# Feed-forward groups in alternating weight order with tiles shared at borders, and Strassen in all second products of layer 2

## The chip, the cores and the metric

One core of a Trainium2 chip (trn2). The metric is device time in microseconds (us) of one execution. TensorE (PE) multiplies, VectorE (DVE) and ScalarE (ACT) work on tiles of 128 partitions, GpSimd (POOL) is idle in the part in question, and SyncE (SP) issues the DMA transfers. Each engine runs its own instructions in the order in which the program was built and waits where an operand or a buffer is not ready.

## The reference, cut to what matters

```
attn = softmax(q k^T / 8 + decay, causal) v      # 4 batches x 8 heads, 576 x 64
x = attn as [2304 tokens, 512]
h = x @ w_in                                     # 512 -> 2048, layer 1
x = (h * sigmoid(1.702 h)) @ w_out               # 2048 -> 512
g = x @ w_gate; v = x @ w_val                    # 512 -> 1536, layer 2
out = (g * sigmoid(g) * v) @ w_out2              # 1536 -> 512
```

All tensors are fp32. Every fp32 operand of a product is split into a high part (a cast to fp32r) and the low rest (a subtraction), and a product is three matmuls: high x high, high x low, low x high.

## The kernel before

**Tiles and stages.** Attention comes first (to about 210 us). The feed-forward part follows: 2304 tokens in three groups of 768, each as two halves of N = 384 columns. Layer 1 has 8 units of 256 hidden columns, layer 2 has 6 units, each with a gate and a value part. Every first product of a unit is one *chain*: the seven products of Strassen-Winograd's scheme, each of six matmuls of 128x128 by 128x384 (lines 750 to 752). The products accumulate in three PSUM tiles called c1, b2 and b3: a new chain's b2 is seeded by an ACT copy of c1 (line 779). PSUM banks are named bank or, where one tile holds two of them, xx.

**The operands of a chain.** X holds the seven forms of a group's input. At the border from one group to another `xbuild` loads eight blocks, makes the sums with 8 DVE subtractions (line 711) and then the 14 high parts on ACT (line 724) and 14 low parts on DVE (line 725). `stream` loads the two weight tiles of a chain, A (384 KB) and B (512 KB), into one of two buffers each (wA, wB), with a cast on ACT (line 684) and a subtraction on DVE (line 685). The weights in memory were prepared before by `prepare` (lines 616 to 651; line 616 is its first ACT step): each unit once, ranked AHEAD (100) before the unit's first use.

**What follows a chain.** `gate` and `value` collect c1, b2, b3 with ACT copies (line 770), DVE additions (line 773), Silu on ACT (lines 813 to 821) and products on DVE (lines 832 to 836). `rounded` splits the result into high and low parts (lines 841 and 842).

**The second products.** They run for a pair of units. `second` is plain: 8 products of 12 matmuls (lines 898 to 900), 96 in all, added into eight fp32 accumulators (line 908 for the first pair, 911 after it). `strassen` does the same by seven products for each of two column blocks: 14 products of 6 matmuls (lines 943 to 945), 84 in all, gathered in PSUM tiles t1, t3, t2 and added by DVE (lines 956 to 960). For it `rounded` first makes the seven forms with four DVE subtractions (line 859) and then splits 7 forms instead of 4. Layer 1 is always plain. In layer 2 group 0 is plain (WHOLE = 1), groups 1 and 2 use Strassen. The weights of the second products come by DMA into a ring of four tiles, wo.

**The order.** A *run* is a stretch of units of one layer and group. Layer 1 goes through the groups twice (units 0 to 3 of groups 0, 1, 2, then units 4 to 7 of 0, 1, 2). Layer 2 has group 0 units 0 to 3, group 1 units 0 to 5, group 2 units 0 to 5, group 0 units 4 and 5. That makes 10 runs and 9 borders. Units always go upward, so the first weights of a run are not those that its predecessor ended with. A group that is left and taken up again has its accumulators saved to memory (yd in layer 1, od in layer 2) and loaded again. The positions of the products in PE's queue come from the patterns ZPAT, WPAT and ZEND; second products start GLAG (plain) or GLAG2 (Strassen) after the pair's last chain. `Program.order` then plans all operations with durations and ranks and emits them in the order of their planned starts, which fixes each engine's queue.

```
    chains = [(1, g, u, "w1") for ps in range(2) for g in range(NG3) for u in range(ps * U1 // 2, (ps + 1) * U1 // 2)]
    runs = [(0, range(0, 4)), (1, range(U2)), (2, range(U2)), (0, range(4, U2))]
    chains += [(2, g, u, k) for g, us in runs for u in us for k in ("wg", "wv")]
```

Of the kernel before, what the change touches and what calls it, by code (L numbers as in the profile page):

```python
# [20 lines left out]
KD = 4  # L21
# [14 lines left out]
DMA_ISSUE, SLACK = 400, 2000  # L36
# [4 lines left out]
EARLY, AHEAD = 8, 100  # L41
SEED, WHOLE = 6, 1
# [3 lines left out]
NB_, NG3 = 384, 3  # L46
# [128 lines left out]
def kernel(  # L175
# [380 lines left out]
    def plain(lay, g):  # L556
        return lay == 1 or g < WHOLE
# [100 lines left out]
    def stream(kind, u, part, rank, stage=None):  # L658
        if part not in ("A", "B"):
            j = ring_of("wO", len(wo))  # L660
            wslot[kind, u, part] = j
            if kind == "w2o":
# [10 lines left out]
        j = ring_of("w" + part, len(ws))  # L673
        wslot[kind, u, part] = j
        if stage is None:
# [122 lines left out]
    def gate(lay, g, u, pos, half):  # L798
        w = 4 if plain(lay, g) else 7
        b_ = buffer(half, w)  # L800
# [44 lines left out]
    def rounded(lay, g, u, t):  # L845
        b_, at_ = made[lay, g, u]
        r = rk(t) - 40
# [131 lines left out]
    for i in range(2, len(chains) + 1):  # L979
        lead1 = i < len(chains) and chains[i][0] == 1  # L980
        whole = not lead1 and chains[min(i, len(chains) - 1)][1] < WHOLE
        pat = (1, -5, 0, 2, -3, 0, 6, -4, 0, 7, 0) if lead1 else WPAT if whole else ZEND if i > len(chains) - 5 else ZPAT
        for m in pat:
# [5 lines left out]
            else:  # L989
                j = i if m > 0 else i - 1  # L990
                if 2 <= j < len(chains):
# [3 lines left out]
                    if m == -4 and kind != "wg" and u % 2:  # L995
# [8 lines left out]
    for i, (lay, g, u, kind) in enumerate(chains):  # L1004
        need.setdefault((kind, u), pos[i][1])
        if kind != "wg" and u % 2:
            for k in range(2):
                need.setdefault(("w1o" if lay == 1 else "w2o", u - k), placed[i][0])
# [15 lines left out]
    for i, (lay, g, u, kind) in enumerate(chains):  # L1024
        events.append((pos[i][1], 2, "chain", i))
        if kind != "wg":
            events.append((pos[i][4] + MP, 1, "round", i))
            if u % 2:
# [3 lines left out]
    def group(lay, g, u, *_):  # L1032
        return lay, g, u >= 4 if lay == 1 or g == 0 else False

    groups = list(dict.fromkeys(group(*c) for c in chains))

# [26 lines left out]
    for t, _, what, arg in events:  # L1063
        if what == "chain":
            lay, g, u, kind = chains[arg]
            gi = groups.index(group(lay, g, u))
# [4 lines left out]
            else:  # L1071
                early = u % 4 < 2 if lay == 1 else u < (2 if g == 0 else 3) or u == 4 and g == 0
# [95 lines left out]
```

## Time and profile before

| what | value |
| --- | --- |
| median of 3 runs | 1009.05 us (1008.55 to 1009.98) |
| the profiled execution's own time | 1006.06 us |
| its span in the trace | 1004.4 us |
| PE busy | 969.6 us (97%), 6593 matmuls |
| DVE busy | 804.3 us (80%) |
| ACT busy | 583.6 us (58%) |
| POOL busy | 120.8 us (12%), all of it in attention |

The span is what the trace covers; the execution's own time has 1.66 us more around it, and the median lies 2.99 us above that execution. Sums on rows of the trace are made against 1006.06. Busy time of an engine is the sum of its instructions without overlaps. An idle stretch in brackets says how long the engine stood still just before an instruction, and which event ended it. What a stall costs is seen from start to start of matmuls, since the matmul after a stall takes longer and the one behind it starts later.

### The profile page before, as it was taken

What the parts mean: (1) busy time and instruction counts of PE and PEld (TensorE: products, weight loads), DVE (VectorE), ACT (ScalarE), POOL (GpSimd) and SP (SyncE); (2) the same over time, 40 slices, a digit from 0 to 9 for tenths busy, and PEclk for the clock granted to TensorE, in tenths of its full rate; (3) what the DMA queues carried; (4) which work ended last, traced back from release to release, by engine and by line L of the source; (5) the groups of instructions that cost most, each with busy time, mean ns of one, the idle gap of its engine ahead of it and who ended that gap; (6) DMA issues with size and microseconds to landing.
All of it is one profiled execution on the core that took longest, in us unless ns stands there. A gap on an engine that the chain in (4) does not pass through costs nothing.

```text
span 1004.4 us, 18051 instructions
## 1 busy us (share of the span) xinstructions
PE 969.6 (97%) x6593; PEld 908.1 (90%) x6593; DVE 804.3 (80%) x1509; ACT 583.6 (58%) x1017; POOL 120.8 (12%) x239
## 2 busy tenths in 40 slices
PE   5999999999999999999999999999999999999998
PEld 4677766779999999999999999999999999999998
DVE  6878778968886797787887988886999987778953
ACT  5556667568656576555554655663667564555730
POOL 4756666400000000000000000000000000000000
PEclk9999999999999999999999999999999999999999
DMA  6567679787977979877869688798687748565327
GB/s 214 171 193 242 223 209 324 214 271 239 310 250 246 302 265 357 298 243 274 311 216 338 243 267 289 256 339 276 205 317 236 238 157 288 173 214 178 100 80 277
DMA packets 137258, 247.14 MB, mean 246 GB/s; under 512 B 13616, under 2 KB 84272, under 8 KB 137168
## 3 DMA queue, kind: packets, MB, share of 16 engines
q1 hardware_dynamic: 137168, 245.97, 73.5%
q8 instruction: 52, 0.85, 0.3%
q14 instruction: 38, 0.31, 0.1%
HBM read 185.81 MB, written 60.01 MB: 245 GB/s over the span
## 4 chain that ended last, share of the span: by engine, by line
PE 78%; DVE 8%; ACT 5%; DMA 4%; issue 3%; POOL 1%; SPq 1%; DVEq 0%; ACTq 0%; POOLq 0%
PE bank L750 8%; PE bank L752 8%; PE bank L751 8%; PE bank L899 6%; PE bank L898 6%; PE bank L900 6%; PE bank L430 4%; PE xx L750 4%; PE xx L752 4%; PE xx L751 4%; PE xx L460 3%; PE bank L943 2%; PE bank L945 2%; PE bank L944 2%; PE bank L364 2%
## 5 line engine op out<-in xcount | busy, mean ns | idle before, releaser
L750 PE MATMUL bank<-X,wB 128*128 128x384 f32 x352 | 118.4, 336 | 1.9 <-ACT FT L770 1.5
L752 PE MATMUL bank<-X,wB 128*128 128x384 f32 x352 | 117.9, 335 | 0.9 <-DVE wB L685 0.9
L751 PE MATMUL bank<-X,wB 128*128 128x384 f32 x352 | 117.6, 334 | 0.0
L898 PE MATMUL bank<-arena,wo 128*128 128x384 f32 x338 | 112.9, 334 | 0.0
L900 PE MATMUL bank<-arena,wo 128*128 128x384 f32 x338 | 112.9, 334 | 0.0
L899 PE MATMUL bank<-arena,wo 128*128 128x384 f32 x338 | 112.9, 334 | 0.0
L750 PE MATMUL bank<-X,wA 128*128 128x384 f32 x248 | 83.4, 336 | 2.2 <-ACT bank L779 1.1
L752 PE MATMUL bank<-X,wA 128*128 128x384 f32 x248 | 83.1, 335 | 0.4 <-DVE wA L685 0.4
L751 PE MATMUL bank<-X,wA 128*128 128x384 f32 x248 | 82.9, 334 | 0.0
L435 ACT ACTIVATE arena<-bank 128x512 f32<-128x512 f32 (+2 forms) x128 | 56.0, 510 | 30.4 <-PE bank L430 22.0
L439 POOL TENSOR_SCALAR_AFFINE_SELECT arena<-arena 128x128 f32<-128x128 f32 (+1 forms) x160 | 64.3, 431 | 71.8 <-ACT arena L435 70.8
L685 DVE TENSOR_TENSOR wB<-arena,wB 128x1024 fp32r<-128x1024 f32 x58 | 70.8, 1221 | 1.0 <-ACT wB L684 1.0
L750 PEld LDWEIGHTS bank<-X,wB 128*128 128x128 f32 x352 | 66.1, 188 | 4.1 <-ACT FT L770 2.8
L372 DVE CUSTOM_DVE_ANT_0 bank<-bank,maskw 128x512 f32<-128x512 f32 (+3 forms) x128 | 59.3, 520 | 13.0 <-PE bank L367 9.5
L752 PEld LDWEIGHTS bank<-X,wB 128*128 128x128 f32 x352 | 66.1, 188 | 1.5 <-DVE wB L685 1.5
L751 PEld LDWEIGHTS bank<-X,wB 128*128 128x128 f32 x352 | 66.1, 188 | 0.0
L430 PEld LDWEIGHTS bank<-arena 64*128 64x128 f32 x768 | 56.9, 188 | 9.2 <-issue 6.5
L684 ACT CAST wB<-arena 128x1024 fp32r<-128x1024 f32 x58 | 61.1, 1053 | 6.8 <-DMA arena<-d_wv_B 4.8
L898 PEld LDWEIGHTS bank<-arena,wo 128*128 128x128 f32 x338 | 63.4, 188 | 0.0
L899 PEld LDWEIGHTS bank<-arena,wo 128*128 128x128 f32 x338 | 63.4, 188 | 0.0
L900 PEld LDWEIGHTS bank<-arena,wo 128*128 128x128 f32 x338 | 63.4, 188 | 0.0
L430 PE MATMUL bank<-arena 64*128 64x192 f32 (+4 forms) x768 | 61.6, 309 | 0.0
(214 smaller groups left out, 2587.4 us busy)
## 6 DMA issues: line engine op xcount, KB each, us to landing
wo<-d_w1o SPq DMA_DIRECT2D x48, 512.0 KB
wo<-d_w2o SPq DMA_DIRECT2D x48, 512.0 KB
arena<-d_w_B SPq DMA_DIRECT2D x22, 512.0 KB
arena<-in_kq_dram SPq DMA_DIRECT2D x16, 576.0 KB
arena<-d_wg_B SPq DMA_DIRECT2D x18, 512.0 KB
arena<-d_wv_B SPq DMA_DIRECT2D x18, 512.0 KB
arena<-d_w_A SPq DMA_DIRECT2D x22, 384.0 KB
yd<-arena SPq DMA_DIRECT2D x42, 192.0 KB
```

The lines of the kernel that those rows point to most:

```text
L372: nc.vector.tensor_tensor_reduce(out=b_, in0=b_, in1=maskw[:, end - n:end], scale=1.0, scalar=floor, op0=ALU.add, op1=ALU.max, accum_out=m ...
L430: nc.tensor.matmul(bank[e][:, o:o + n], w[half[e]], x[half[e]], start=i == 0, stop=i == 3)
L435: nc.scalar.activation(out=ps[e][:, a:z], in_=bk("sc", P, c, e)[:, 0:z - a], func=AF.Exp, scale=0.125)
L439: nc.gpsimd.affine_select(out=q, in_=q, pattern=[[1, q.shape[1]]], compare_op=ALU.is_ge, fill=0.0, base=0, channel_multiplier=-1)
L684: add("act", 220 + .83 * n, rank + 4, lambda: nc.scalar.copy(out=t[:, :, :, 0, :], in_=s), K, W)
L685: add("dve", 145 + 1.04 * n, rank + 5, lambda: nc.vector.tensor_tensor(out=t[:, :, :, 1, :], in0=s, in1=f32(t[:, :, :, 0, :]), op=ALU.subt ...
L750: nc.tensor.matmul(o_, w_[:, 0, :], x_[:, 0, :], start=start and h == 0, stop=False, skip_group_check=True)
L751: nc.tensor.matmul(o_, w_[:, 0, :], x_[:, 1, :], start=False, stop=False, skip_group_check=True)
L752: nc.tensor.matmul(o_, w_[:, 1, :], x_[:, 0, :], start=False, stop=h == 1 and stop, skip_group_check=True)
L898: nc.tensor.matmul(o_, w[0], gt[:, 0, :], start=q == 0, stop=False)
L899: nc.tensor.matmul(o_, w[0], gt[:, 1, :], start=False, stop=False)
L900: nc.tensor.matmul(o_, w[1], gt[:, 0, :], start=False, stop=q == len(tiles) - 1)
```

## The change

The order of runs becomes a table, RUNS, of 9 runs with 8 borders. Neighbouring runs of a layer meet at the same units: where a run ends with units 2, 3 the next begins with 3, 2, or it ends with 7 and the next begins with 7. `keep` remembers what lies in the buffers of wA, wB and wo. Where the wanted tile is still there `stream` loads nothing and reuses it; otherwise it replaces the tile used longest ago. PLAIN is empty, so group 0 of layer 2 uses Strassen too. A group whose run comes back later still saves and loads its accumulators (`mode` and `closed` in the diff). AHEAD goes from 100 to 60, so the weights are prepared later by rank. LATE gives 300 ns of slack to loads ranked past 99 in the plan. `buffer` picks places for a unit's results that no live unit holds.

```diff
@@ constants
-EARLY, AHEAD = 8, 100
-SEED, WHOLE = 6, 1
+EARLY, AHEAD = 8, 60
+SEED = 6
+RUNS = (((1, 0), (0, 1, 2, 3)), ((1, 1), (3, 2, 1, 0)), ((1, 2), (0, 1, 2, 3, 4, 5, 6, 7)), ((1, 1), (7, 6, 5, 4)), ((1, 0), (4, 5, 6, 7)),
+        ((2, 2), (0, 1, 2, 3)), ((2, 1), (3, 2, 1, 0, 4, 5)), ((2, 2), (5, 4)), ((2, 0), (4, 5, 0, 1, 2, 3)))
+PLAIN = ()
...
-        add("sp", issue, rank, lambda: nc.sync.dma_start(out=o, in_=i), reads, writes, lat=lat, after=after, size=n, slack=slack)
+        add("sp", issue, rank, lambda: nc.sync.dma_start(out=o, in_=i), reads, writes, lat=lat, after=after, size=n, slack=max(slack, LATE if rank > 99 else 0))
...
     def plain(lay, g):
-        return lay == 1 or g < WHOLE
+        return lay == 1 or g in PLAIN
...
-    turns = {(1, 7): 1}
-
-    def buffer(half, n):
+    turns, live = {}, {}
+
+    def buffer(half, n, at):
+        m = len(at)
         i = turns.get((half, n), 0)
+        while any(15 * half + at[i % m] < z and a < 15 * half + at[i % m] + n for a, z in live.values()):
+            i += 1
+            assert i < turns.get((half, n), 0) + m
         turns[half, n] = i + 1
-        return 15 * half + n * (i % (3 if n == 4 else 2))
+        return 15 * half + at[i % m]
...
+    held = {}
+
+    def keep(name, n, key):
+        l = held.setdefault(name, [(None, i) for i in range(n)])
+        j = next((q for q in range(n) if l[q][0] == key), None)
+        found = j is not None
+        _, i = l.pop(j if found else 0)
+        l.append((key, i))
+        return i, found
...
     def stream(kind, u, part, rank, stage=None):
         if part not in ("A", "B"):
-            j = ring_of("wO", len(wo))
+            j, found = keep("wO", len(wo), (kind, u, part))
             wslot[kind, u, part] = j
+            if found:
+                return
...
-        j = ring_of("w" + part, len(ws))
+        j, found = keep("w" + part, len(ws), (kind, u))
         wslot[kind, u, part] = j
+        if found:
+            return
...
-    chains = [(1, g, u, "w1") for ps in range(2) for g in range(NG3) for u in range(ps * U1 // 2, (ps + 1) * U1 // 2)]
-    runs = [(0, range(0, 4)), (1, range(U2)), (2, range(U2)), (0, range(4, U2))]
-    chains += [(2, g, u, k) for g, us in runs for u in us for k in ("wg", "wv")]
+    chains, meta, events_of = [], [], {}
+    for n, ((lay, g), us) in enumerate(RUNS):
+        for q, u in enumerate(us):
+            for kind in (("w1",) if lay == 1 else ("wg", "wv")):
+                shut_ = kind != "wg" and u // 2 in [x // 2 for x in us[:q]]
+                if shut_:
+                    events_of.setdefault(n, []).append(len(chains))
+                chains.append((lay, g, u, kind))
+                meta.append((n, q, shut_))
...
+            mode = "first" if opened and not before else "mid" if not closed else "save" if after and lay == 2 else "last"
+            (second if plain(lay, g) else strassen)(lay, g, (u // 2 * 2, u // 2 * 2 + 1), mode, w)
```

Counted over the built programs, the change has 36 matmuls less (96 fewer each in lines 898 to 900, 84 more each in lines 943 to 945), 14 loads less of A and of B each, each with its cast and subtraction, one rebuild of X less, 24 subtractions of line 859 more, 16 loads of layer 1's second weights less, 8 saves and 8 loads of yd less, 12 loads for Strassen pairs more, and 56 DMAs less in all.

The first place is ACT at the start of the fourth run of layer 1, with lines of each program (745, 705, 863 and 800 of the change are 724, 684, 841 and 779 of before; wA_65 and wB_66 are the weight tiles, arena_62 and FT fp32 scratch, arena_61 and g_72 split operands). Before:

```order
L724 CAST X<-arena_62 128x384 x2
L684 CAST wB_66<-arena_62 128x8x128
L821 ACTIVATE FT<-FT 128x768
L841 CAST g_72<-FT 128x2x384
L908 ACTIVATE arena_62<-bank_89 128x384
L841 CAST arena_61<-FT 128x384
L724 CAST X<-arena_62 128x384 x2
L616 ACTIVATE pre<-arena_62 128x2x512
L908 ACTIVATE arena_62<-bank_90 128x384
L684 CAST wA_65<-arena_62 128x6x128
L779 COPY bank_88<-xx 128x384
```

And with the change:

```order
L745 CAST X<-arena_62 128x384 x2
L835 ACTIVATE FT<-xx 128x384
L863 CAST arena_61<-FT 128x384
L791 COPY FT<-bank_85 128x384
L745 CAST X<-arena_62 128x384 x2
L843 ACTIVATE FT<-FT 128x768
L863 CAST arena_61<-FT 128x2x384
L863 CAST arena_61<-FT 128x384
L745 CAST X<-arena_62 128x384 x2
L633 ACTIVATE pre<-stg 128x2x512
L800 COPY xx<-xx 128x384
```

In place of the two weight casts (line 684) and the accumulators' first writes (line 908) stand casts of X and the splitting of results only.

The second place is DVE at the border into the last run of Strassen units, before into group 2, with the change into group 0 (lines 746, 794, 858, 882, 864 of the change are 725, 773, 836, 859, 842 of before). Before:

```order
L773 TENSOR_TENSOR arena_62<-arena_62,bank_90 128x384
L859 TENSOR_TENSOR arena_62<-arena_62 128x384
L836 TENSOR_TENSOR arena_62<-arena_62 128x2x384
L725 TENSOR_TENSOR X<-FT,X 128x384
L859 TENSOR_TENSOR arena_62<-arena_62 128x384 x2
L725 TENSOR_TENSOR X<-FT,X 128x384
L773 TENSOR_TENSOR arena_62<-arena_62,xx 128x384
L834 TENSOR_TENSOR arena_62<-arena_62,bank_87 128x384
L859 TENSOR_TENSOR arena_62<-arena_62 128x384
L725 TENSOR_TENSOR X<-FT,X 128x384 x2
L842 TENSOR_TENSOR arena_61<-arena_62,arena_61 128x4x384
L842 TENSOR_TENSOR g_72<-arena_62,g_72 128x2x384
```

With the change:

```order
L794 TENSOR_TENSOR arena_62<-arena_62,bank_90 128x384
L746 TENSOR_TENSOR X<-FT,X 128x384
L858 TENSOR_TENSOR arena_62<-arena_62 128x2x384
L882 TENSOR_TENSOR arena_62<-arena_62 128x384 x2
L856 TENSOR_TENSOR arena_62<-arena_62,xx 128x384
L882 TENSOR_TENSOR arena_62<-arena_62 128x384
L746 TENSOR_TENSOR X<-FT,X 128x384
L732 TENSOR_TENSOR FT<-FT 128x384
L864 TENSOR_TENSOR arena_61<-arena_62,arena_61 128x3x384 x2
L746 TENSOR_TENSOR X<-FT,X 128x384
```

The splitting of the left unit (842, 864) keeps its place behind the four subtractions, and two X sums (732, before 711) and single X subtractions have come between them.

The third place is SP at the tail, where the last weights of a Strassen pair are fetched into wo (d_w2o is the prepared weight, out_dram the result; line 285 is 282 of before). Before:

```order
L282 DMA wo_68<-d_w2o_138 128x512
L282 DMA wo_69<-d_w2o_138 128x512
L282 DMA wo_70<-d_w2o_138 128x1024
L282 DMA out_dram<-arena_62 128x384
L282 DMA wo_71<-d_w2o_138 128x1024
L282 DMA out_dram<-arena_62 128x384
L282 DMA wo_68<-d_w2o_138 128x1024
L282 DMA out_dram<-arena_62 128x384
L282 DMA wo_69<-d_w2o_138 128x1024
L282 DMA out_dram<-FT 128x384
```

With the change:

```order
L285 DMA wo_68<-d_w2o_137 128x512
L285 DMA wo_69<-d_w2o_137 128x512
L285 DMA wo_70<-d_w2o_137 128x1024
L285 DMA out_dram<-arena_62 128x384
L285 DMA wo_71<-d_w2o_137 128x1024
L285 DMA out_dram<-arena_62 128x384 x2
L285 DMA out_dram<-FT 128x384
L285 DMA out_dram<-arena_62 128x384 x4
```

The loads of the plain second products (wo_68, wo_69 behind the first stores) are gone, and only stores follow the pair's last tile.

## Rows read from the trace of the kernel before

**Rows 1.** page, parts 1, 2: busy us (share) xinstructions; clock in 40 slices.
```profile
PE 969.6 (97%) x6593; PEld 908.1 (90%) x6593; DVE 804.3 (80%) x1509; ACT 583.6 (58%) x1017; POOL 120.8 (12%) x239
PEclk9999999999999999999999999999999999999999
```

**Rows 2.** stretches: us, busy of PE, PEld, DVE, ACT, POOL, clock, DMA, GB/s.
```profile
215.00:1001.00 786.00, 772.32 (x4412) 763.40 (x4410) 634.96 (x1014) 454.66 (x767) 0.00 (x0) 1.00 0.75 252
780.00:800.00 20.00, 19.71 (x113) 19.07 (x112) 20.00 (x35) 10.44 (x17) 0.00 (x0) 1.00 0.81 243
```

**Rows 3.** PE's timeline, tail: start, us, engine line op out<-in [idle before].
```profile
974.38 0.33 PE L943 MATMUL bank<-arena,wo 128*128 128x384 f32 x1
...
977.33 0.34 PE L945 MATMUL xx<-arena,wo 128*128 128x384 f32 x1
978.85 0.41 PE L943 MATMUL bank<-arena,wo 128*128 128x384 f32 x1 [1.19 <-DMA wo<-d_w2o]
...
981.87 0.41 PE L943 MATMUL xx<-arena,wo 128*128 128x384 f32 x1 [0.67 <-DVE arena L960]
```

**Rows 4.** waits of PE from 215 to 1005: total us, times, longest us.
```profile
PE xx L750 <- ACT xx L779: 2.2, 4, 0.6
...
PE bank L750 <- ACT bank L779: 1.1, 2, 0.6
```

**Rows 5.** PE's timeline around 435 us.
```profile
435.01 0.34 PE L752 MATMUL xx<-X,wB 128*128 128x384 f32 x1
435.90 0.45 PE L750 MATMUL xx<-X,wA 128*128 128x384 f32 x1 [0.55 <-ACT xx L779]
436.18 0.34 PE L751 MATMUL xx<-X,wA 128*128 128x384 f32 x1
```

**Rows 6.** ACT's timeline around 435 us.
```profile
435.38 0.46 ACT L779 COPY xx<-bank 128x384 f32<-128x384 f32 x1 [2.86 <-PE xx L752]
```

**Rows 7.** PE's timeline behind four borders, and at 611.77.
```profile
308.49 0.45 PE L750 MATMUL xx<-X,wB 128*128 128x384 f32 x1 [0.74 <-ACT arena L908]
...
369.55 0.45 PE L898 MATMUL xx<-arena,wo 128*128 128x384 f32 x1 [1.48 <-ACT bank L779]
...
511.61 0.45 PE L750 MATMUL xx<-X,wB 128*128 128x384 f32 x1 [0.71 <-DVE arena L911]
...
571.20 0.44 PE L750 MATMUL bank<-X,wB 128*128 128x384 f32 x1 [0.21 <-ACT arena L770]
...
611.77 0.41 PE L750 MATMUL xx<-X,wB 128*128 128x384 f32 x1 [1.81 <-ACT pre L616]
```

**Rows 8.** ACT's timeline just before 369.55 us.
```profile
366.87 1.15 ACT L616 ACTIVATE pre<-arena 128x1024 f32<-128x1024 f32 x1
...
368.27 0.84 ACT L684 CAST wA<-arena 128x768 fp32r<-128x768 f32 x1
```

**Rows 9.** groups by shape: count | busy us, mean ns | idle before.
```profile
L685 DVE TENSOR_TENSOR wB<-arena,wB 128x1024 fp32r<-128x1024 f32 x58 | 70.8, 1221 | 1.0 <-ACT wB L684 1.0
...
L684 ACT CAST wB<-arena 128x1024 fp32r<-128x1024 f32 x58 | 61.1, 1053 | 6.8 <-DMA arena<-d_wv_B 4.8 <-DMA arena<-d_wg_B 1.2 <-PE bank L751 0.7
...
L685 DVE TENSOR_TENSOR wA<-arena,wA 128x768 fp32r<-128x768 f32 x58 | 55.3, 955 | 0.8 <-ACT wA L684 0.6
...
L684 ACT CAST wA<-arena 128x768 fp32r<-128x768 f32 x58 | 48.7, 840 | 0.8 <-PE bank L751 0.4 <-PE xx L751 0.4
...
L725 DVE TENSOR_TENSOR X<-FT,X 128x384 fp32r<-128x384 f32 x70 | 36.7, 559 | 8.1 <-ACT X L724 5.6 <-DMA arena<-da 2.5
...
L724 ACT CAST X<-FT 128x384 fp32r<-128x384 f32 x70 | 33.1, 518 | 2.7 <-DMA FT<-xd 2.6
...
L842 DVE TENSOR_TENSOR arena<-arena,arena 128x1152 fp32r<-128x1152 f32 x6 | 8.2, 1359 | 1.7 <-ACT arena L841 1.7
```

**Rows 10.** SP's timeline, the issue of a weight load at the tail.
```profile
974.57 0.32 SPq L282 DMA_DIRECT2D wo<-d_w2o  x1
```

**Rows 11.** DVE's timeline at 814 us: two X subtractions in a row.
```profile
814.00 1.02 DVE L725 TENSOR_TENSOR X<-FT,X 128x384 fp32r<-128x384 f32 x2
```

More of the change, by code (lines that the diff above doesn't have):

```diff
@@ L35 @@
 SAME = dict(pe=0, dve=100, act=0, pool=0, sp=0)
[L36 removed]
+DMA_ISSUE, SLACK, LATE = 400, 2000, 300
 DMA_RATE, DMA_WAIT = 300, 1900
@@ L799, in gate @@
         w = 4 if plain(lay, g) else 7
-        b_ = buffer(half, w)
+        b_ = buffer(half, w, (0, 4, 8) if lay == 1 else (0, 8) if w == 4 else (0, 7))
+        live[lay, g, u] = b_, b_ + w
         at_ = [b_ + q for q in ((0, 1, 2, 3) if plain(lay, g) else (0, 6, 3, 5))]
@@ L846, in rounded @@
         b_, at_ = made[lay, g, u]
+        del live[lay, g, u]
         r = rk(t) - 40
@@ L980 @@
         lead1 = i < len(chains) and chains[i][0] == 1
-        whole = not lead1 and chains[min(i, len(chains) - 1)][1] < WHOLE
+        whole = not lead1 and chains[min(i, len(chains) - 1)][1] in PLAIN
         pat = (1, -5, 0, 2, -3, 0, 6, -4, 0, 7, 0) if lead1 else WPAT if whole else ZEND if i > len(chains) - 5 else ZPAT
@@ L994 @@
                     lay, g, u, kind = chains[j]
-                    if m == -4 and kind != "wg" and u % 2:
+                    if m == -4 and meta[j][2]:
                         waiting += [(t + (GLAG if plain(lay, g) else GLAG2), j, SP_ if plain(lay, g) else MP)] * (8 if plain(lay, g) else 14)
@@ L1005 @@
         need.setdefault((kind, u), pos[i][1])
-        if kind != "wg" and u % 2:
+        if meta[i][2]:
             for k in range(2):
-                need.setdefault(("w1o" if lay == 1 else "w2o", u - k), placed[i][0])
+                need.setdefault(("w1o" if lay == 1 else "w2o", u // 2 * 2 + k), placed[i][0])
     todo = sorted(need, key=lambda k: (need[k], k[1]))
@@ L1031 @@
     seconds = [e[3] for e in events if e[2] == "second"]
-    def group(lay, g, u, *_):
-        return lay, g, u >= 4 if lay == 1 or g == 0 else False
-    groups = list(dict.fromkeys(group(*c) for c in chains))
     def stream_chain(i):
@@ L1065 @@
             lay, g, u, kind = chains[arg]
-            gi = groups.index(group(lay, g, u))
+            gi, q, _ = meta[arg]
             if arg:
@@ L1071 @@
             else:
-                early = u % 4 < 2 if lay == 1 else u < (2 if g == 0 else 3) or u == 4 and g == 0
-                if lay == 2 and plain(lay, g) and u in (2, 4):
-                    turns[0, 4] = 1 if u == 2 else 0
+                early = q < min(2 if plain(lay, g) else 3, len(RUNS[gi][1]) // 2)
                 gate(lay, g, u, pos[arg], gi % 2 if not early or gi == 0 else 1 - gi % 2)
-            if arg + 1 < len(chains) and chains[arg + 1][:2] != (lay, g):
+            if arg + 1 < len(chains) and meta[arg + 1][0] != gi:
                 l2, g2 = chains[arg + 1][:2]
@@ L1084 @@
             lay, g, u, _ = chains[i]
[L1085 to L1103 removed]
+            n_ = meta[i][0]
+            opened, closed = i == events_of[n_][0], i == events_of[n_][-1]
+            before = [m for m in range(n_) if RUNS[m][0] == (lay, g)]
+            after = [m for m in range(n_ + 1, len(RUNS)) if RUNS[m][0] == (lay, g)]
+            if opened and before:
+                for d in range(KD):
+                    for n in range(2):
+                        c = g * 2 * N + n * N
+                        if lay == 1:
+                            sp(rk(w[0]) - 25, acc[2 * d + n], yd[d, :, c:c + N], [("yd", g, d, n)], [("acc", 2 * d + n)], 3000)
+                        else:
+                            sp(rk(w[0]) - 25, acc[2 * d + n], od[d, :, n * N:(n + 1) * N], [("od", d, n)], [("acc", 2 * d + n)], 3000)
+            mode = "first" if opened and not before else "mid" if not closed else "save" if after and lay == 2 else "last"
+            (second if plain(lay, g) else strassen)(lay, g, (u // 2 * 2, u // 2 * 2 + 1), mode, w)
             nsec += 1
```

19 lines of the change are left out of this document (1 added, 18 removed).

## The prediction

> **What bounds the kernel now.** I read the page's busy shares first, then the clock, then the window of the feed-forward part, then where TensorE (PE) loses time inside it. The reader is to see PE busy 97% of the span, DVE 80%, ACT 58%, and the granted clock at its upper level, 2.4 GHz, in every slice [rows 1]. The edit touches only the feed-forward part. From 215 to 1001 us PE is busy 772.32 of 786.00 us, with DVE at 634.96 and ACT at 454.66 [rows 2]. So PE is the bound there, and its pace comes from its timeline: from the matmul at 974.38 to the one at 977.33, 17 steps without a gap, one takes 2.95 / 17 = 0.1734 us [rows 3]. 4412 matmuls at that pace need 765 us; the remaining 21 us are stalls. A changed kernel can therefore gain in two ways: fewer matmuls, or fewer stalls.
>
> The stalls are of three kinds. The first I call seed waits: six of them, four with xx and two with bank as the released tile [rows 4]. In the one at 435.90 PE has finished the last product of a chain in one half of xx at 435.01 + 0.34; only then does ACT's copy of bank c1 into the other half of xx start, at 435.38 after 2.86 us idle [rows 5, 6]. The two halves are one tile, so the copy waits for a product it has nothing to do with. Start to start PE loses 0.89 - 0.17 = 0.72, and the next matmul comes 0.28 - 0.17 = 0.11 late: 0.83 for a wait shown as 0.55, that is 0.28 over the wait shown [rows 5]. The second kind stands at the borders of layer 1: 0.74, 1.48, 0.71 and 0.21 us, and at 611.77 one of 1.81 behind a weight preparation [rows 7]. At the longest of the four ACT works off a backlog of a preparation (1.15) and a weight cast (0.84) just ahead of the copy that PE wants [rows 8]. The third is the tail: 1.19 for a weight DMA and 0.67 shown as DVE [rows 3].
>
> **The change, part by part.**
>
> Strassen in group 0 of layer 2: three pairs of units, each 8 products of 12 matmuls before and 14 of 6 now, so 3 x (96 - 84) = 36 matmuls fewer. At 0.1734 this is **-6.2 us**, all on PE's own path. The Trainium skill ("TensorE: Matmul & The Clock Gate", section "Back-to-back issue gap") has a warm matmul follow another after N / 2.4 ns plus about 2.5. For N = 384 that would be an estimated 162.5 ns and -5.9 us; the trace says 173.4 and decides.
>
> What Strassen adds is on DVE: 4 subtractions for each of 6 units, 24 x 0.56 = 13.3 us, and the rounding of 7 forms instead of 4, 3 x 384 more columns for 6 units at 1.36, 8.2 us, with at most as much on ACT [rows 9]. I cost both at nothing: the cover is PE's products, and DVE loses more elsewhere. If that cover were gone, all 21.5 us would show, which is the worst end of this term.
>
> Sharing: the alternating order has 8 borders and 9 runs instead of 9 and 10, and at borders the two buffers of wA and of wB already hold the first units' tiles. Counting instructions, 14 A loads and 14 B loads go, 12.5 MB. With each goes an ACT cast (0.840 and 1.053) and a DVE subtraction (0.955 and 1.221): 14 x 1.893 = 26.5 us of ACT and 14 x 2.176 = 30.5 us of DVE [rows 9]. One rebuild of X goes too: 14 casts of 0.52 on ACT, 22 subtractions of 0.56 on DVE (7.3 and 12.3), and its 8 loads from the queue of SP. DVE's net is -30.5 - 12.3 + 21.5 = -21 us. None of this is PE time by itself; what it brings is fewer stalls at the borders. A border in layer 1 loses two pairs of tiles, 3.8 us of ACT and 4.4 us of DVE. The four waits there cost 3.14 + 4 x 0.28 = 4.3 us [rows 7], and the weight cast in front of the longest one (0.84) is among what goes [rows 8]. So the ends of this term are 0 and -4.3. I take **-3.0**, nearer the far end: the backlog removed (3.8) is larger than the longest wait, but X's casts stay in the same queue. The wait at 611.77 I leave as it is.
>
> Seed waits: in the program's order the pattern that causes one (seed copy into the half of xx next to a half PE is filling, with PE's next product on it) comes up 4 times instead of 6: 2 x 0.83 = **-1.7 us**.
>
> A new wait at the border from run (2,2) with units 5, 4 to run (2,0). There the first accumulation of the next pair needs the 3-form rounding of unit 4. Four products of six matmuls (4.2 us) stand between the end of unit 4's last product and it. Behind that product DVE has ten instructions in its queue up to and with that rounding: eight of 384 columns at 0.56, one of 768 at 0.95 (taken as the A subtraction, of the same size) and the rounding of 1152 at 1.36 [rows 9], 6.8 us. Each starts some 0.1 before the one ahead ends, as two in a row take 1.02 and not 1.12 [rows 11]: 5.9. 5.9 - 4.2 = 1.7, and with 0.28 for the late restart I take **+2.0 us**. Ends: 0, if DVE runs the interleaved X subtractions early, and 4, if it comes to this place with a backlog. Queued behind it are all later products of PE.
>
> The tail: the last pair still has only three products between the last use of a weight buffer and the product that wants its refill, and the refill is issued at 974.57, and PE restarts at 978.85 [rows 3, 10]. The order of the change has the same three there, with one store issued between the two refills as now, so that wait stays. The second wait (0.67 + 0.28) gives way to another: four DVE instructions stand between the two products into t3 of a pair with one product beside them, 4 x 0.56 = 2.2 against 1.04, about 1.2 us. That is +0.2; as the old one may stay too, I take **+0.5**, ends -1 and +2. The Trainium skill ("DMA: Bandwidth & Descriptors", section on the anatomy of one DMA) gives, for DMAs issued by GpSimd, 2.0 us and the bytes over 436 GB/s. For 512 KB that is an estimated 3.2 us, and the wait at 978.85 would be about 0.3; this queue is SP's, the trace has 4.28 from issue to restart, and I go by it.
>
> Fewer loads of weights for the second products (w1o, 48 to 32) and 8 saves and loads of y fewer take DMA issues from SP; its queue is named in no wait but the tail's, so I count nothing. Preparing the weights 40 us later is ranked, not timed, and is costed at nothing; its price if wrong is the second rival.
>
> **Sum**: -6.2 - 3.0 - 1.7 + 2.0 + 0.5 = **-8.4 us**. The profiled execution took 1006.06, so 997.7 there. The median of the runs, 1009.05, lies 2.99 above that execution; I carry the difference over, 1009.05 - 8.4 = **1000.6 us**. 0.2%, about what a measurement of this kernel can tell from no change, is 2.0 us.
>
> **The rivals.**
>
> *All border waits go.* With DVE 21 us and ACT some 27 us lighter, the waits of layer 1 and the one at 611.77 (1.81 + 0.28) go in full and the new wait does not come: -6.2 - 4.3 - 2.1 - 1.7 = -14.3, or 994.8. For it: each border wait names ACT or DVE behind a backlog [rows 7]. Against: the X casts stay in ACT's queue, and DVE is full in stretches, 20.00 of 20 us from 780 to 800 [rows 2], so a backlog can still form. Chance 0.13, from -11 to -16.
>
> *Preparation too late.* Ranked 40 us later, the preparations fall into busier stretches, and waits like that at 611.77 (2.1 with its 0.28) come two or three times: +4 to +6 on the sum, -2 to -5, about 1005. For it: the trace has one such wait even with the earlier rank. Against: preparing less early also takes a rival for ACT away at the first borders [rows 8]. Chance 0.13.
>
> *DVE becomes the bound at the last border* (slower). At (2,2) to (2,0) stand 14 X subtractions and 8 sums (22 x 0.56 = 12.3) and the Strassen subtractions and rounding of two units (8 x 0.56 + 2 x about 3.3 = 11.1): 23 us of DVE in about as much PE time, on top of its normal 80%. Before, group 0 came to its last run with plain products. If more than 8.4 us of it is uncovered the gain is gone; with 2 to 10 more than that the time is 1011 to 1019, I say 1013. Against it: in the stretch where DVE was full PE still ran 19.71 of 20 us [rows 2], so a full DVE alone does not stop PE. Chance 0.08.
>
> *Shared tiles and fewer products change nothing measurable*: waits take back what the matmuls gave, within 2.0 us, 1009. For it only that the waits I can name (2.0 + 0.5) could be thrice as large. Chance 0.06.
>
> **How the numbers follow.** Forecast (-5 to -11) 0.60, all border waits 0.13, late preparation 0.13, no change 0.06, slower 0.08. Faster 0.60 + 0.13 + 0.13 = 0.86, same 0.06, slower 0.08. The range leaves out the last two and the fastest corner: from 994.0 (the first rival with all its terms, a little under 994.8) to 1007.0 (late preparation at -2).
>
> **What would show it.** PE's matmul count 36 lower with the same pace; 14 casts fewer for wA and wB each; four seed waits; no waits over 0.5 at layer 1's borders; one wait of about 2 us at the start of the last run, with a rounding as releaser; about 2.5 to 3 us lost in the tail. I am wrong in mechanism if the stalls in the window grow by more than 3 us, if several waits name a preparation, or if DVE's busy time does not fall by about 20 us.

## The result and the profile after

The change takes 1000.46 us in the median of 4 runs (999.39 to 1001.17), beside 1009.51 us for the kernel before on the same chip: a ratio of 0.9913, 95% interval [0.9897, 0.9928], 7 to 10 us faster. The forecast was 1000.6 us, with 994.0 to 1007.0.

Part 1 of the page of the change, and the stretch from 215 us to the end of the feed-forward part (columns as in [rows 2]):

```profile
PE 964.5 (97%) x6557; PEld 903.0 (90%) x6557; DVE 790.5 (79%) x1495; ACT 564.0 (56%) x981; POOL 121.0 (12%) x239
```

```profile
215.00:995.00 780.00, 767.28 (x4385) 758.69 (x4383) 623.88 (x1004) 435.89 (x732) 0.00 (x0) 1.00 0.69 227
```

Against [rows 1] PE has 36 matmuls fewer, and DVE 13.8 us less, not 21. Against [rows 2], 4385 matmuls at 0.1734 us are 760.4 us, so 19.6 us of the 780 are stalls, where before had 21.0. Matmuls and stalls give -6.2 - 1.4 = -7.6 us for this stretch, and I had forecast -8.4.

The profiled executions differ by less, 1006.06 and 1000.45. Stretches of 2 us in attention, where the queues of PE, DVE, ACT and POOL are the same in both kernels, tell part of the reason. First the change, then before:

```profile
166.00:168.00 2.00, 0.59 (x4) 0.34 (x6) 1.52 (x2) 2.00 (x7) 0.07 (x1) 1.00 1.02 413
168.00:170.00 2.00, 2.00 (x12) 0.81 (x8) 2.00 (x4) 1.19 (x2) 0.00 (x0) 0.56 1.03 419
170.00:172.00 2.00, 2.00 (x22) 2.00 (x20) 1.18 (x3) 0.87 (x3) 0.29 (x1) 0.58 1.01 398
```

```profile
166.00:168.00 2.00, 0.82 (x5) 0.34 (x6) 1.72 (x3) 2.00 (x6) 0.21 (x1) 1.00 1.02 412
168.00:170.00 2.00, 2.00 (x24) 1.49 (x22) 2.00 (x4) 1.28 (x3) 0.00 (x0) 1.00 1.04 420
```

In both PE stands still for more than 1 us between 166 and 168. In the execution of the change the granted clock then is 0.56 and 0.58 for 4 us, so most of them at the lower level of 1.2 GHz, and 2 x 0.44 + 2 x 0.42 = 1.7 us are lost; in that of before it stays at 1.00. Seven of the kernels below have the same queues up to 200 us. Of the nine profiled executions three lost clock there: the change after a wait of 1.53 us, early_prep after 1.97 and no_share_ab after 2.05. The other six stayed at 1.00, after waits of 0.46 to 1.61 us (before 1.18, late_pairs 1.61). So the 5.6 us between the two profiles hold one such event, which kernels with these queues have in some profiles and not in others, and the medians are the better measure. The other half of the gap to the medians' 9 us is in no row: before's profiled execution was itself 3.45 us under its median.

Three of the longest groups of PE's waits in the change from 205 us on, one at the start and two of seed waits (total us, times, longest us); the others stand with their rows further down:

```profile
PE bank L771 <- ACT FT L791: 2.7, 2, 1.4
...
PE xx L771 <- ACT xx L800: 1.2, 2, 0.6
...
PE bank L771 <- ACT bank L800: 1.1, 2, 0.6
```

### The profile page after: what moved, and what is told of

It reads as the page before. It is cut to its first block, busy times and chain, and to the rows that moved or that the text cites. A ratio compares the mean times of both kernels' runs of the same rounds, so it can differ in the third digit from the quotient of the medians.

```text
span 998.7 us, 17848 instructions
## 1 busy us (share of the span) xinstructions
PE 964.5 (97%) x6557; PEld 903.0 (90%) x6557; DVE 790.5 (79%) x1495; ACT 564.0 (56%) x981; POOL 121.0 (12%) x239
## 4 chain that ended last, share of the span: by engine, by line
PE 88%; DVE 5%; ACT 3%; DMA 2%; issue 1%; POOL 0%; SPq 0%; ACTq 0%; DVEq 0%; POOLq 0%
PE bank L771 9%; PE bank L773 9%; PE bank L772 9%; PE bank L923 6%; PE bank L922 6%; PE bank L921 6%; PE xx L771 5%; PE xx L773 5%; PE xx L772 5%; PE bank L433 5%; PE xx L463 4%; PE bank L967 3%; PE bank L966 3%; PE bank L968 3%; PE xx L493 2%; PE bank L367 2%
## 5 line engine op out<-in xcount | busy, mean ns | idle before, releaser
L771 PE MATMUL bank<-X,wB 128*128 128x384 f32 x344 | 115.3, 335 | 0.6 <-ACT FT L791 0.6
L773 PE MATMUL bank<-X,wB 128*128 128x384 f32 x344 | 115.1, 334 | 0.0
L772 PE MATMUL bank<-X,wB 128*128 128x384 f32 x344 | 114.9, 334 | 0.0
L922 PE MATMUL bank<-arena,wo 128*128 128x384 f32 x322 | 107.6, 334 | 0.0
L923 PE MATMUL bank<-arena,wo 128*128 128x384 f32 x322 | 107.6, 334 | 0.0
L921 PE MATMUL bank<-arena,wo 128*128 128x384 f32 x322 | 107.6, 334 | 0.0
L771 PE MATMUL bank<-X,wA 128*128 128x384 f32 x202 | 68.2, 337 | 4.1 <-ACT FT L791 2.7
L773 PE MATMUL bank<-X,wA 128*128 128x384 f32 x202 | 67.8, 336 | 0.5 <-DVE wA L706 0.4
L772 PE MATMUL bank<-X,wA 128*128 128x384 f32 x202 | 67.5, 334 | 0.0
L771 PEld LDWEIGHTS bank<-X,wB 128*128 128x128 f32 x344 | 64.6, 188 | 1.2 <-ACT FT L791 0.9
L773 PEld LDWEIGHTS bank<-X,wB 128*128 128x128 f32 x344 | 64.6, 188 | 0.3 <-DVE wB L706 0.3
L772 PEld LDWEIGHTS bank<-X,wB 128*128 128x128 f32 x344 | 64.6, 188 | 0.0
L966 PE MATMUL bank<-arena,wo 128*128 128x384 f32 x181 | 61.0, 337 | 1.6 <-DVE arena L983 0.7
L967 PE MATMUL bank<-arena,wo 128*128 128x384 f32 x181 | 60.7, 335 | 1.5 <-DVE arena L864 1.5
L968 PE MATMUL bank<-arena,wo 128*128 128x384 f32 x181 | 60.5, 334 | 0.0
L922 PEld LDWEIGHTS bank<-arena,wo 128*128 128x128 f32 x322 | 60.4, 188 | 0.0
L921 PEld LDWEIGHTS bank<-arena,wo 128*128 128x128 f32 x322 | 60.4, 188 | 0.0
```

The source lines that it names most:

```text
L771: nc.tensor.matmul(o_, w_[:, 0, :], x_[:, 0, :], start=start and h == 0, stop=False, skip_group_check=True)
L772: nc.tensor.matmul(o_, w_[:, 0, :], x_[:, 1, :], start=False, stop=False, skip_group_check=True)
L773: nc.tensor.matmul(o_, w_[:, 1, :], x_[:, 0, :], start=False, stop=h == 1 and stop, skip_group_check=True)
L921: nc.tensor.matmul(o_, w[0], gt[:, 0, :], start=q == 0, stop=False)
L922: nc.tensor.matmul(o_, w[0], gt[:, 1, :], start=False, stop=False)
L923: nc.tensor.matmul(o_, w[1], gt[:, 0, :], start=False, stop=q == len(tiles) - 1)
```

## The experiments

All ratios are to runs of the kernel before on the same chip in the same job; its medians there were 1007.75, 1008.62 and 1008.12 us.

### strassen_only: the kernel before with Strassen in group 0

```diff
-SEED, WHOLE = 6, 1
+SEED, WHOLE = 6, 0
```

> The kernel before with Strassen in group 0 of layer 2 too (WHOLE = 0), order of runs and weight loads as before. My theory (36 matmuls at 0.1734 count in full, the added 21 us of DVE work is hidden): 36 matmuls fewer, DVE busy up by about 20 us, stalls within 2 us of before's, so 6.2 us less, up to 2 more or less: 1002 to 1005 beside a before of 1009.5. Rival (Strassen's DVE work is what sharing had to make room for): without the shared tiles DVE falls behind in group 0, the stalls grow by 4 us or more, and 1007 to 1010 results.

Measured: 1036.78 us, ratio 1.0288 [1.0263, 1.0313]. Both theories were far off. PE's two longest groups of waits from 205 us on, and one instruction of DVE's timeline:

```profile
PE xx L943 <- DVE arena L960: 5.3, 1, 5.3
PE bank L944 <- DVE arena L842: 4.2, 2, 2.5
```

```profile
1014.82 0.55 DVE L960 TENSOR_TENSOR arena<-arena,xx 128x384 f32<-128x384 f32 x1 [4.57 <-DMA arena<-od]
```

The first wait hangs on the last of these rows. In the order of before group 0 is taken up again as the very last run, and its saved accumulators (od) come back from memory with DVE 4.57 us idle for them; the other is PE waiting for Strassen operands that DVE has not finished. The two are 9.5 of the 29 us. The rest are 24 other waits from 620 us on, the longest 3.5, and three stretches, 20 us in all, at a granted clock of 0.57 (738 to 742, 789 to 797 and 1014 to 1022 us). So in this order the matmuls saved are no gain. This run moves the places of DVE's work too, so it is not a clean price of Strassen.

### share_only: the change with group 0 plain

```diff
-PLAIN = ()
+PLAIN = (0,)
```

> The change with group 0 of layer 2 plain again (PLAIN = (0,)): only the order of the runs and the shared tiles remain. My theory: 36 matmuls back (+6.2 against the change), the wait of 1.51 + 0.51 at the border into group 0 gone (about -2.5), the waits of the tail between the t3 products gone (-1 to -2), the waits of layer 1 gone as with the change: 1002 to 1005, so 4.5 to 7 us under before. Rival (sharing is worth nothing, the matmuls were all of it): 1006.5 to 1009.

Measured: 1003.80 us, 0.9961 [0.9943, 0.9978]. Inside my range, with one step of it wrong:

```profile
PE bank L967 <- DVE arena L864: 1.5, 1, 1.5
```

The wait at the border into group 0 is still there. Its products belong to the last pair of group 2, which is Strassen in both, and not to group 0. Strassen in group 0 is worth the step of the ratio from 0.9961 to 0.9913 (of two jobs), some 4.8 us: 6.2 of matmuls, less what the tail's waits take back. In the profiles part of that is clock. Behind this wait share_only ran 4 us at 0.60, which costs 1.6 us, where the change, behind the same wait, stayed at 1.00:

```profile
848.00:852.00 4.00, 4.00 (x16) 4.00 (x16) 3.06 (x6) 0.51 (x1) 0.00 (x0) 0.60 0.24 66
```

### no_share_ab: the change without sharing wA and wB

```diff
         found = j is not None
+        if name != "wO":
+            found, j = False, None
```

> The change with its order of runs, but wA and wB loaded anew at each border (wo still shared). My theory: casts and subtractions of 14 A and 14 B tiles come back (27 us of ACT, 30 us of DVE), and with them waits at layer 1's borders, up to the 4.3 us of before: 1002.5 to 1005.5 against 1000.5. Rival (the order alone removed the waits, the loads are hidden): 1000 to 1001.5, with no wait over 0.5 us at layer 1's borders.

Measured: 1018.05 us, 1.0088 [1.0066, 1.0110], 17.6 us over the change. Neither theory had that. The price is mainly one wait, at the border of layer 2 into the run (2,2) with units 5 and 4. PE's timeline there, and two stretches around it:

```profile
797.94 0.34 PE L774 MATMUL bank<-X,wA 128*128 128x384 f32 x1
813.11 0.69 PE L775 MATMUL bank<-X,wA 128*128 128x384 f32 x1 [14.83 <-DVE wA L708]
```

```profile
791.00:813.00 22.00, 5.38 (x28) 4.42 (x27) 22.00 (x35) 11.86 (x17) 0.00 (x0) 0.73 0.40 115
813.00:833.00 20.00, 19.88 (x100) 19.57 (x101) 9.82 (x16) 8.72 (x16) 0.00 (x0) 0.87 0.85 289
```

DVE is busy for all 22.00 us of the first stretch, with the rebuild of X, the rounding of a Strassen unit and a weight preparation ahead of the low part of wA that PE waits for. After 14.83 us of waiting the matmuls run below full clock, 0.87 in the mean of the next 20 us, which costs 20 x 0.13 = 2.6 us more. And in layer 1 the view of waits names none for PE between 240 and 608 us, though every weight tile is loaded, cast and subtracted again.

### early_prep: AHEAD back to 100

```diff
-EARLY, AHEAD = 8, 60
+EARLY, AHEAD = 8, 100
```

> The change with weights prepared as early by rank as before (AHEAD 100 in place of 60). The wait of 1.81 behind a preparation at 611.77 is gone in the change. If the later rank removed it, it or another behind line 633 comes back: 1001.5 to 1004. If it was the order of runs that moved it, the time stays within 1 us of the change, 999.5 to 1001.5, and PE waits for no preparation. I hold the second for likelier.

Measured: 1001.58 us (998.97 to 1005.33), 0.9936 [0.9914, 0.9959]. The interval overlaps that of the change, and PE waits for no preparation. The second expectation holds: the later rank did not remove the wait at 611.77.

### old_l1 and old_l1b: layer 1's old orders in the change

```diff
-RUNS = (((1, 0), (0, 1, 2, 3)), ((1, 1), (3, 2, 1, 0)), ((1, 2), (0, 1, 2, 3, 4, 5, 6, 7)), ((1, 1), (7, 6, 5, 4)), ((1, 0), (4, 5, 6, 7)),
+RUNS = (((1, 0), (0, 1, 2, 3)), ((1, 1), (0, 1, 2, 3)), ((1, 2), (0, 1, 2, 3)), ((1, 0), (4, 5, 6, 7)), ((1, 1), (4, 5, 6, 7)), ((1, 2), (4, 5, 6, 7)),
```

In old_l1b the groups stand as 0, 2, 1 in place of 0, 1, 2. In old_l1 layer 2 begins with a group 2 that lacks the last units of layer 1, so it leaves out that part of the sum there and does not wait for it.

> The change with layer 1's runs in the order of before (groups 0, 1, 2 with units 0 to 3, then with 4 to 7, always upward; so few tiles are shared there and there is one border more), layer 2 as in the change. My theory: the waits behind layer 1's borders return (4.3 us as shown in before), and nothing else moves: 1003 to 1006. Rival A (the later preparation removed them, not the order): 1000 to 1001.5. Rival B (layer 1's spared DVE and ACT time is what layer 2 lives on, since layer 2's weights are prepared in it): waits of several us in layer 2, 1008 or more.

> The change with layer 1's units always upward and six runs of four units, as before, but groups in the order 0, 2, 1 twice, so that group 2 is complete when layer 2 begins with it (the run old_l1 began layer 2 with a group 2 whose last pair of units of layer 1 was not yet added). Theory B (layer 1's spared DVE time is what layer 2's weight preparation lives on): waits of several us in layer 2, many of them naming DVE, 20 us or more over the change: 1020 to 1036. Theory A (only layer 1's own border waits are at stake): 1003 to 1006.

Measured: old_l1 1034.83 us, 1.0254 [1.0230, 1.0279]; old_l1b 1028.06 us, 1.0200 [1.0177, 1.0224]. The time and the waits that rival B forecast came in both. In layer 1 old_l1 has two waits (1.81 us at 354.66 and 1.48 at 543.88), and for old_l1b the view again names none between 240 and 608 us. From there on its waits name DVE above all:

```profile
PE bank L773 <- DVE wB L706: 5.9, 3, 2.1
PE bank L772 <- DVE X L746: 5.5, 4, 2.5
```

What moved is the preparation of weights. These are the instructions on the tile pre (the preparation's scratch) from 240 to 580 us, which is layer 1, and from 580 to 860; after the length come DVE's busy time and then ACT's. Before, the change, and old_l1b:

```profile
240.00:580.00 340.00, 85.80 (x117) 23.50 (x21) 1.00 0.81 277
580.00:860.00 280.00, 61.51 (x78) 19.51 (x15) 1.00 0.79 260
```

```profile
240.00:580.00 340.00, 98.59 (x131) 28.13 (x24) 1.00 0.73 240
580.00:860.00 280.00, 47.77 (x65) 14.85 (x11) 1.00 0.73 240
```

```profile
240.00:580.00 340.00, 83.13 (x112) 24.68 (x21) 1.00 0.82 278
580.00:860.00 280.00, 64.01 (x85) 18.20 (x14) 0.96 0.71 239
```

In the change DVE has done 98.6 us of preparation by 580 us, before 85.8, in old_l1b 83.1. What is not done by then falls into layer 2, where Strassen fills DVE: 47.8 us against 61.5 and 64.0. In early_prep, with AHEAD back at 100, it is 98.0 by 580 us, so the order moved it and not the rank. That the moved preparation is what old_l1b pays for is read from these rows; no run moved it alone. Part of the price is clock, too: 0.90 in the mean from 765 to 890 us, where the change has 1.00, so an estimated 12 of the 28 us at most (125 x 0.10).

### split, late_pairs and both: shared PSUM tile and short lag

split, in short (attention's copy of 576 columns becomes one of 448 and one of 128):

```diff
-    xx = pm.tile([128, 1024], F32, name="xx")
-    bank += [xx[:, 0:512], xx[:, 512:1024]]
+    xa = pm.tile([128, 512], F32, name="xa")
+    xb = pm.tile([128, 512], F32, name="xb")
+    bank += [xa[:, :], xb[:, :]]
```

late_pairs:

```diff
-GLAG, GLAG2 = 10000, 4000
+GLAG, GLAG2 = 10000, 8000
```

both has split's edit with GLAG2 9000 and LATE 0; LATE 0 was not tried by itself.

> The change with xx as two PSUM tiles of one bank each (one copy in attention becomes two, 16 times). My theory: the four seed waits of 0.55 us, in which ACT's copy of c1 waits for products in the other half of xx, go, and each gave back 0.83 us: 3.3 us less than the change, 996 to 998.5; no wait of PE that names a copy between halves of one tile is left. Rival (the waits come from ACT's queue and not from the shared tile, or attention pays for 16 more copies of about 0.3 us): 1000 to 1003.

> The change with the Strassen second products placed 4 us later behind their last chain (GLAG2 8000 in place of 4000). My theory: the wait at the border into group 0 (0.51 + 1.51) and those between the t3 products of the tail come from too little time between a chain's end and the first product on its rounded forms; both fall by half or more: 2 to 4 us less than the change, 996.5 to 998.5. Rival (DVE has no time to spare there, so the wait follows the products wherever they stand): 999.5 to 1002.

> The change with xx in two tiles, the Strassen second products 5 us later (GLAG2 9000) and no slack for late loads in the plan (LATE 0). If seed waits and short lags are two causes of their own, their gains add: 3.3 + 2 to 4 less than the change, 993 to 995.5. Rival (what one gives back the other's waits take): the time of the better of the two alone, 996 to 998.5.

Measured: split 988.42 us, 0.9799 [0.9786, 0.9813]; late_pairs 993.46 us, 0.9853 [0.9839, 0.9866]; both 984.34 us, 0.9765 [0.9750, 0.9781]. All three beat their expectation.

split: no wait between halves of one tile is left, and most of the gain came where I had not looked. Waits of PE in attention, 20 to 200 us, of the change and of split:

```profile
PE xx L463 <- ACT arena L498: 3.7, 7, 1.5
```

```profile
PE xb L468 <- ACT arena L502: 0.6, 1, 0.6
```

Attention's copies out of one half of xx had held up PE's products into the other half. Matmul number 2129, the same place of PE's queue in all these kernels, where attention ends, comes at 201.06 us in split and at 207.66 in late_pairs, whose attention is that of the change: 6.6 us, beside the 3.3 that I had expected for the seed waits.

late_pairs: the wait at the border shrank less than I expected.

```profile
843.24 0.45 PE L966 MATMUL bank<-arena,wo 128*128 128x384 f32 x1 [0.75 <-ACT arena L863]
844.63 0.45 PE L967 MATMUL bank<-arena,wo 128*128 128x384 f32 x1 [0.95 <-DVE arena L864]
```

0.75 + 0.95 in place of 0.51 + 1.51: the products were placed later, but DVE's queue had shifted too, so here the rival is nearly right. The rest of the gain are waits between 667 and 785 us, at 874.85 and in the tail, which are gone or half as long, but for the one for a DMA at the end (1.35). In both, the gains add in part: 4 us under split, and 984.34 us is the fastest version of this study, 24 us under before. PE's longest waits from 205 us on are now

```profile
PE bank L777 <- ACT FT L797: 1.6, 2, 1.0
PE bank L777 <- DVE FT L800: 1.3, 2, 1.1
PE bank L972 <- DMA wo<-d_w2o: 1.2, 1, 1.2
```

### both_plain0 and both_noshare: the two parts, priced where few stalls are left

They are both with PLAIN = (0,), and both with no_share_ab's edit. In both_plain0 one operand of group 0's first pair is overwritten by a later unit's before its late products read it (seven tiles, two to a unit); the number of its instructions is unchanged.

> The kernel of the run called both, with group 0 of layer 2 plain again (PLAIN = (0,)). Here few stalls are left, so the price of 36 matmuls should show by itself. Theory (0.1734 us a matmul, Strassen's added DVE work hidden): 6.2 us more, less the 1 to 2.5 us that its tail waits cost: 988 to 991 against 984.3. Rival (DVE's relief of 21 us gives as much back as the matmuls cost): within 1.5 us of 984.3.

> The kernel of the run called both, with wA and wB loaded anew at each border. Theory (sharing is needed where the rebuild of X, the Strassen roundings and a weight preparation meet on DVE, at layer 2's last borders, whatever the copies and lags are): a wait of 5 us or more there again and 8 to 16 us more than 984.3, so 992 to 1000. Rival (the 14.83 us of the run without sharing came from the shared PSUM tile or the short lag): under 4 us more, 984 to 988.

Measured: both_plain0 986.66 us, 0.9785 [0.9768, 0.9802]; both_noshare 998.34 us, 0.9897 [0.9878, 0.9915]. Strassen in group 0 is worth 2.3 us here, between theory and rival. The 36 matmuls are there, 6.2 us; but from 205 us to the last matmul, less 0.1734 us for each, the plain kernel has 7.1 us of stalls against 8.6, and its matmul number 2129 starts at 200.45 us against 202.61, for a reason that I found only in part: 1.3 us of that lead are there at matmul number 71 (22.43 us against 23.72), at the very start of the program. From number 2129 to the last one the plain kernel takes 780.61 us against 775.75. So there Strassen is worth 4.9 us, of which 1.7 are clock again (0.57 from 837 to 841 us in the plain kernel, 1.00 in both). Without the clock that leaves about 3 us here. The same sum between share_only and the change is 789.67 - 785.89 - 1.6, so about 2. Sharing is worth 14 us, mainly at the border that no_share_ab showed:

```profile
806.06 0.69 PE L781 MATMUL bank<-X,wB 128*128 128x384 f32 x1 [8.21 <-DVE wB L714]
```

### before_split: the kernel before with two tiles for xx

> The kernel before with xx as two tiles and nothing else. If the shared tile costs the same in both programs (in attention some 7.5 us, in the feed-forward part six seed waits of 0.83, 5 us), this gives 10 to 13 us less than before, 996 to 999, and the change's own gain stays what it was, on top. Rival (before's plan falls into another jam): 1000 to 1008.

Measured: 1001.89 us (998.05 to 1004.07), 0.9928 [0.9906, 0.9950]: 6 us by the medians, 7 by the ratio, which is the rival's range. Attention gains as in split (number 2129 at 201.55 us against 207.22), but a new wait takes a good part of the rest back:

```profile
788.93 0.69 PE L757 MATMUL bank<-X,wA 128*128 128x384 f32 x1 [5.17 <-DVE X L731]
```

And there is more in this run than its time. It has before's order, every weight cast of before and the old rank, yet from 230 to 750 us the view of waits names none for PE. The four waits behind layer 1's borders [rows 7] are gone, and so is the one at 611.77. Four of these five stood in front of a product into xx.

## Why the prediction was right, and where its reasons were not

The sum held by the medians, at 1000.46 against 1000.6. By the profiled executions it did not quite: 1000.45 came where I had put 997.7. Of these 2.75 us 1.7 are the lost clock in attention and 0.8 the terms. Its terms, in PE's time between 215 us and the end, with 0.28 added to each wait as in the prediction:

| term | forecast | in the profile |
| --- | --- | --- |
| 36 matmuls | -6.2 | -6.2 |
| seed waits | -1.7 | -1.6 (four left) |
| waits behind layer 1's borders | -3.0 (0 to -4.3) | -4.3 |
| wait at 611.77 | 0 | -2.1 |
| border into group 0 | +2.0 (0 to 4) | 0.51 + 1.51 + 0.56 = +2.6 |
| tail | +0.5 (-1 to +2) | 4.6 - 2.4 = +2.2 |
| not named: +0.6 at the start, +0.5 at 927.41, the rest in no wait of the view | 0 | +1.8 |

**Right in mechanism and size: matmuls, seed waits, the border into group 0.** The pace is unchanged: from 845.81 to 846.16 two steps take 175 ns each, at the two digits of the rows. The estimate of 162.5 ns by the Trainium skill ("TensorE: Matmul & The Clock Gate", section "Back-to-back issue gap") is not borne out here either. The seed waits are four as the order said (497.29, 559.50, 667.93 and 756.81 us). The border wait came as counted. PE's rows there, and DVE's queue from the addition behind unit 4's last product to its rounding:

```profile
845.81 0.33 PE L966 MATMUL bank<-arena,wo 128*128 128x384 f32 x1
...
846.16 0.34 PE L968 MATMUL bank<-arena,wo 128*128 128x384 f32 x1
847.01 0.44 PE L966 MATMUL bank<-arena,wo 128*128 128x384 f32 x1 [0.51 <-ACT arena L863]
848.96 0.44 PE L967 MATMUL bank<-arena,wo 128*128 128x384 f32 x1 [1.51 <-DVE arena L864]
```

```profile
842.82 0.55 DVE L794 TENSOR_TENSOR arena<-arena,bank 128x384 f32<-128x384 f32 x1
843.28 0.55 DVE L746 TENSOR_TENSOR X<-FT,X 128x384 fp32r<-128x384 f32 x1
843.75 0.95 DVE L858 TENSOR_TENSOR arena<-arena 128x768 f32<-128x768 f32 x1
844.74 1.03 DVE L882 TENSOR_TENSOR arena<-arena 128x384 f32<-128x384 f32 x2
845.68 0.55 DVE L856 TENSOR_TENSOR arena<-arena,xx 128x384 f32<-128x384 f32 x1
846.15 0.55 DVE L882 TENSOR_TENSOR arena<-arena 128x384 f32<-128x384 f32 x1
846.62 0.55 DVE L746 TENSOR_TENSOR X<-FT,X 128x384 fp32r<-128x384 f32 x1
847.08 0.55 DVE L732 TENSOR_TENSOR FT<-FT 128x384 f32<-128x384 f32 x1
847.55 2.62 DVE L864 TENSOR_TENSOR arena<-arena,arena 128x1152 fp32r<-128x1152 f32 x2
```

These are the ten instructions of the prediction, in its order, the first of the last two being the one that PE needs. From 842.82 to PE's restart at 848.96 they took 6.1 us, and I had forecast 5.9.

**Right way, wrong size: the tail.** I put the wait between the t3 products at 1.2 us, and it was 1.12, but I let it replace the one at 981.87. It came beside two more and the DMA wait of 1.29, for a load issued at 986.07. The prediction's estimate of 3.2 us a load from the Trainium skill ("DMA: Bandwidth & Descriptors", section "Anatomy of one DMA — SWDGE (gpsimd) path"), given there for DMAs issued by GpSimd, would have put that wait near 0.3; from issue to restart it took 4.38 here:

```profile
972.58 0.44 PE L966 MATMUL xx<-arena,wo 128*128 128x384 f32 x1 [1.12 <-DVE FT L983]
...
979.51 0.44 PE L966 MATMUL bank<-arena,wo 128*128 128x384 f32 x1 [0.42 <-ACT bank L979]
...
982.64 0.44 PE L966 MATMUL bank<-arena,wo 128*128 128x384 f32 x1 [0.67 <-DVE arena L983]
...
990.45 0.41 PE L966 MATMUL xx<-arena,wo 128*128 128x384 f32 x1 [1.29 <-DMA wo<-d_w2o]
```

**A gap in the sum of DVE.** "DVE's net is -30.5 - 12.3 + 21.5 = -21 us" left out that Strassen also gathers its products: 28 additions more in line 960 and 16 fewer in line 911, 12 x 0.55 = 6.6 us. With it -14.7 is expected, and -13.8 was measured. I had named a fall of less than about 20 us as a sign of a wrong mechanism; it was a sign of this count. The casts and subtractions of the weights went as counted, from 58 to 44 each:

```profile
L706 DVE TENSOR_TENSOR wB<-arena,wB 128x1024 fp32r<-128x1024 f32 x44 | 53.6, 1218 | 1.0 <-ACT wB L705 1.0
...
L705 ACT CAST wB<-arena 128x1024 fp32r<-128x1024 f32 x44 | 46.4, 1055 | 4.0 <-PE bank L772 2.9 <-DMA arena<-d_wv_B 0.7 <-PE xx L772 0.4
```

**The step that failed** is "what it brings is fewer stalls at the borders", that is "A border in layer 1 loses two pairs of tiles, 3.8 us of ACT and 4.4 us of DVE" as the cause of -3.0. In no_share_ab all those casts and subtractions are back, and layer 1 has no wait; in old_l1b the order of units is the old one, and it has none either. before_split has none with before's own order and all of its casts. Those waits are small collisions of particular plans. Of the plans with the new table only old_l1 has such, and in before's own plan splitting the shared tile was enough to be rid of them. The runs put something larger in that place: at layer 2's last borders DVE has to have room, and without the sharing it has not, which costs 14 us (both_noshare) or 17.6 (no_share_ab). The trace shows two possible sources of that room. DVE may make fewer low parts at the border itself, and the planner puts more of the weight preparation into layer 1: 98.6 us by 580 us, where no_share_ab has 93.8 and old_l1b 83.1. How the 14 us divide between the two was not tried, but the traces weigh them. These are the instructions on pre from 780 to 820 us, the stretch of that border, in the change, both, no_share_ab and both_noshare:

```profile
780.00:820.00 40.00, 2.02 (x1) 0.00 (x0) 1.00 0.60 191
780.00:820.00 40.00, 0.00 (x0) 0.00 (x0) 1.00 0.64 196
780.00:820.00 40.00, 9.50 (x10) 2.81 (x2) 0.79 0.59 177
780.00:820.00 40.00, 7.54 (x9) 2.56 (x2) 0.91 0.72 225
```

Without sharing DVE has 7.5 us more of preparation there, in either pair. Low parts of wA and wB are 4.34 us in the change and 4.33 in no_share_ab, 4.32 in both and 7.38 in both_noshare. So what stands in the way at the border is above all a preparation that came late. The amount done by 580 us does not decide it: split has 95.7, no more than both_noshare with 96.1, but is done by 780 us and has no such wait. No run moved the preparation alone, so this stays a reading of the traces. Which single part of the new order took away the wait at 611.77 stays open too.

**The rival that I gave 0.08**, DVE as the bound at layer 2's last border, does not happen in the change. But no_share_ab is it nearly to the letter: 22.00 of 22 us of DVE, PE at a stand, 1018 us where I had put 1011 to 1019. One border earlier than I said, and what decides is the sharing. The change as a whole is safe only with it. That Strassen in group 0 is what needs it is not shown: the stall lies ahead of group 0's run, between groups that had Strassen before, and no run went without sharing and with group 0 plain in this order. The late preparation that I gave 0.13 cost nothing (early_prep).

A forecast whose terms were off by -1.3, -2.1, +0.1, +0.6, +1.7 and +1.8 us and that came out 0.14 us from the median was also lucky. The terms as measured add up to -7.6, and the medians moved by some 9 us; the rest no row explains.

## What to carry to other kernels

Where PE is busy 97% of the time, count PE's work first, then ask which engine has the least room in the stage where work is added. Relief elsewhere may be what lets that stage keep up, as a planner moves work across stages. And look for one tile with two owners: two PSUM banks in one tile cost the change 12 us and the kernel before 6, where the whole change brought 9. The rows that show it are a copy that waits for products in the half that it does not touch, and products that wait for a copy out of the other half.

## What the hardware showed that I had not expected

A wait of 1.53 us of PE in attention was followed by 4 us at a granted clock of 0.56 to 0.58 in the change, and one of 1.61 us at the same place by none in late_pairs. At the border into group 0 the same pair of waits (0.5 and 1.5 us) was followed by 4 us at 0.60 in share_only and by 1.00 in the change. After 14.83 us of waiting, the mean clock was 0.87 over 20 us. So a stall can cost more than its length, and at these lengths whether it does differs from execution to execution.

It is one source of the spread between executions of one kernel, and not the main one. Of before's eleven executions in the last job the one with a mean clock of 1.000 was the shortest (1005.31 us), but the eight at 0.998 went from 1006.29 to 1010.09. Late_pairs at 0.998 to 1.000 stayed within 993.18 to 993.87. Where the rest of before's spread comes from the profiles do not tell.
